# Attention in 512-token chunks inside a rational feed-forward: one activation table set, and the numerator as four matmul terms

## The chip, the cores and the metric

The kernel runs on one core of a Trainium2 chip. The time is device microseconds of the whole program; the kernel before takes 825.4 us (median; 824.55 to 825.59). Some executions fall into a slower state, with a lower granted clock and a longer time; comparisons are between runs of the fast state, unless a text says otherwise. Each ratio is to the kernel before on the same chip and in the same rounds. The twelve experiments ran on four chips, so one experiment set against another may cross chips; the kernel before had medians of 825.00 to 825.28 us on all four. Ratios are the mean time of one kernel's fast runs over that of the other's fast runs of the same rounds, so they are not quite the ratio of the medians quoted beside them.

Engine names in the profile: PE is the matmul engine (PEld its weight loads), ACT is ScalarE, DVE is VectorE, POOL is GpSimd, SP starts the DMAs.

## The reference, cut to what matters

A polynomial-sketch linear attention (batch 4, 4 heads, 1088 positions, head size 32, sketch rank 8) is followed by a feed-forward with a rational activation (4352 tokens, 128 -> 2048 -> 128).

```
phi(x) = outer(S1 x, S2 x), flattened to 64 features
kv = sum over positions of phi(k) v ;  z = sum of phi(k)
x  = (phi(q) kv) / (phi(q) z + 1e-6)              # per head, heads side by side: 128 wide
h  = x @ w_in
P  = a0 + a1 h + a2 h^2 + a3 h^3
Q  = 1 + |b0| |h| + |b1| h^2
out = (P / (Q + 1e-6)) @ w_out
```

1/Q is formed as Exp(-Ln(Q)) in both kernels.

## The kernel before

Attention comes first, in tiles of 128 positions: all keys, then all queries. Its last step writes x, transposed, for all tokens. Then the feed-forward runs in tiles of 1024 tokens, 16 blocks of 128 hidden units each:

```python
for fi in range(nf):
    h_ps = ...                                            # two f32 matmuls of 512 columns
    hh  = copy(h_ps)                                      # ACT, to bf16
    h2  = hh * hh                                         # DVE
    t1  = a1 * hh + a0 ; P3 = a3 * hh + a2                # DVE
    nc.scalar.activation(out=habs, in_=hh, func=ACT.Abs, scale=ab0)
    P   = P3 * h2 + t1                                    # DVE, two instructions
    Qp  = ab1 * h2 + habs                                 # DVE, two instructions
    nc.scalar.activation(out=Qln, in_=Qp, func=ACT.Ln, bias=one_ap)
    nc.scalar.activation(out=Qr, in_=Qln, func=ACT.Exp, scale=-1.0)
    g   = P * Qr                                          # DVE
    out_ps += w_out[fi] x g                               # two bf16 matmuls of 512 columns
```

(Shortened; a scheduler then fixes the order of each engine's instructions before the program runs.)

## Time and profile before

| stage | us | ACT busy | DVE busy | PE busy |
|---|---|---|---|---|
| attention | 0 to 305 | 30% | 36% | 64% |
| feed-forward | 305 to 824 | 97% | 60% | 54% |

The two windows behind the table (length, busy us and count of PE, PEld, DVE, ACT and POOL, granted clock, DMA share, GB/s):

```profile
0.00:305.00 305.00, 196.51 (x746) 132.31 (x746) 110.47 (x251) 91.41 (x388) 9.91 (x55) 1.00 0.17 29
305.00:824.00 519.00, 280.87 (x466) 102.33 (x466) 311.78 (x641) 503.29 (x517) 0.00 (x0) 0.66 0.02 5
```

From the page of the kernel before: the busy lines, and three of the rows that cut the span in 40 slices (each digit is a busy share in tenths; PEclk is the clock granted to PE).

```profile
PE 477.4 (58%) x1212; PEld 234.6 (28%) x1212; DVE 422.3 (51%) x892; ACT 594.7 (72%) x905; POOL 9.9 (1%) x55
...
PE   3888965666565546465665656664555545643331
...
ACT  2222433333332219999999999999999999999997
PEclk9999999999999998777776665567766578555555
...
ACT 57%; PE 21%; issue 10%; DVE 9%; DMA 2%; SPq 0%; ACTq 0%
```

The break at slice 15 is the end of attention. Behind it ACT is full and PE is not, and PE's clock wanders between half and full. The last line is the chain of work that ended last, by engine: more than half of it is ACT.

From the groups of instructions (busy us, mean ns of one), the two lines of table loads:

```profile
L247 ACT ACT_TABLE_LOAD x79 | 101.4, 1283 | 1.5
L245 ACT ACT_TABLE_LOAD x79 | 101.4, 1283 | 1.5
```

And from the timeline, ACT alone, one beat of the feed-forward (start us, duration us, instruction):

```profile
506.84 1.28 ACT L245 ACT_TABLE_LOAD   x1
508.13 1.15 ACT L245 ACTIVATE Qln<-Qp,one_ap 128x1024 bf16<-128x1024 bf16 x1
509.19 1.13 ACT L237 ACTIVATE habs<-hh,b_abs 128x1024 bf16<-128x1024 bf16 x1
510.34 1.28 ACT L247 ACT_TABLE_LOAD   x1
511.63 1.06 ACT L247 ACTIVATE Qr<-Qln 128x1024 bf16<-128x1024 bf16 x1
512.60 0.99 ACT L229 CAST hh<-h_ps 128x1024 bf16<-128x1024 f32 x1
513.61 1.28 ACT L245 ACT_TABLE_LOAD   x1
```

From load to load the beat is 513.61 - 506.84 = 6.77 us, with no gap; 2.56 us of it are two table loads, because Ln and Exp are taken from different sets.

### The profile page before, as it was taken

Reading aid. Unit: us, or ns where it says so; the run is one execution under the profiler, and the core shown is the slowest. Engines: PE = TensorE matmul, PEld = TensorE weight load, DVE = VectorE, ACT = ScalarE, POOL = GpSimd, SP = SyncE. Lnnn points to the kernel's source line nnn. Section 1 sums busy time; section 2 is a strip of 40 time slices with the busy share of each in tenths; the row PEclk is TensorE's granted clock in tenths of the full one; section 3 lists DMA queues with packets and bytes.
Section 4 is the critical chain, followed back from the end, with each engine's and each line's share of the span. In section 5 each row is a group of like instructions: output and inputs, shape, how many; then the busy total and the mean of one; then the engine's idle time right before and its main releaser. Section 6 shows DMA issues by size and latency. Waiting matters only on the chain.

```text
span 824.1 us, 5057 instructions
## 1 busy us (share of the span) xinstructions
PE 477.4 (58%) x1212; PEld 234.6 (28%) x1212; DVE 422.3 (51%) x892; ACT 594.7 (72%) x905; POOL 9.9 (1%) x55
## 2 busy tenths in 40 slices
PE   3888965666565546465665656664555545643331
PEld 2766733333332222121222212221111212211110
DVE  0111344344434446666566665665656666566333
ACT  2222433333332219999999999999999999999997
POOL 3000000000000000000000000000000000000000
PEclk9999999999999998777776665567766578555555
DMA  6333210000000000000000000000000000000000
GB/s 147 59 59 59 33 28 13 8 11 13 5 0 1 0 0 0 1 0 0 0 6 20 0 1 0 0 20 6 0 0 2 13 13 0 0 0 1 19 7 6
DMA packets 59869, 11.34 MB, mean 14 GB/s; under 512 B 54848, under 2 KB 59200, under 8 KB 59712
## 3 DMA queue, kind: packets, MB, share of 16 engines
q1 hardware_dynamic: 59840, 11.02, 7.1%
q8 instruction: 10, 0.16, 0.1%
q14 instruction: 19, 0.16, 0.1%
HBM read 8.79 MB, written 2.23 MB: 13 GB/s over the span
## 4 chain that ended last, share of the span: by engine, by line
ACT 57%; PE 21%; issue 10%; DVE 9%; DMA 2%; SPq 0%; ACTq 0%
ACT L245 12%; ACT L247 11%; ACT Qln L245 10%; ACT Qr L247 8%; ACT hh L229 7%; PE nd_ps L183 5%; DVE denb L197 3%; PE ab_ps L126 3%; ACT xT L188 3%; DVE denb L190 3%; ACT habs L237 2%; PE rden_ps L199 2%; PE q_pT L175 2%; PE ab_ps L165 2%; DVE q_p L169 1%
## 5 line engine op out<-in xcount | busy, mean ns | idle before, releaser
L226 PE MATMUL h_ps<-xT,w_in_sb 128*128 128x512 f32 (+1 forms) x288 | 226.1, 909 | 140.8 <-ACT hh L229 140.4
L226 PEld LDWEIGHTS h_ps<-xT,w_in_sb 128*128 128x128 f32 x288 | 78.1, 293 | 251.9 <-ACT hh L229 205.5
L249 DVE TENSOR_TENSOR g<-P,Qr 128x1024 bf16<-128x1024 bf16 (+1 forms) x80 | 49.0, 612 | 195.7 <-ACT Qr L247 195.7
L252 PE MATMUL out_ps<-g,w_out_sb 128*128 128x512 bf16 (+1 forms) x144 | 66.1, 548 | 81.1 <-DVE g L249 81.0
L188 ACT COPY xT<-nd_ps 32x128 f32<-32x128 f32 (+1 forms) x144 | 35.9, 249 | 105.0 <-PE nd_ps L183 78.1
L247 ACT ACT_TABLE_LOAD x79 | 101.4, 1283 | 1.5
L245 ACT ACT_TABLE_LOAD x79 | 101.4, 1283 | 1.5
L190 DVE COPY denb<-nd_ps 1x128 f32<-1x128 f32 (+1 forms) x144 | 40.6, 282 | 84.6 <-ACT xT L188 83.1
L245 ACT ACTIVATE Qln<-Qp,one_ap 128x1024 bf16<-128x1024 bf16 (+1 forms) x80 | 81.5, 1020 | 2.3 <-DVE Qp L243 1.4
L237 ACT ACTIVATE habs<-hh,b_abs 128x1024 bf16<-128x1024 bf16 (+1 forms) x80 | 80.7, 1008 | 0.1
L247 ACT ACTIVATE Qr<-Qln 128x1024 bf16<-128x1024 bf16 (+1 forms) x80 | 74.1, 928 | 0.9
L229 ACT CAST hh<-h_ps 128x1024 bf16<-128x1024 f32 (+1 forms) x80 | 68.9, 869 | 6.6 <-PE h_ps L226 6.6
L183 PE MATMUL nd_ps<-q_pT_sb,kv_blk 128*128 128x128 f32 (+1 forms) x144 | 52.4, 467 | 21.3 <-DVE denb L190 21.3
L252 PEld LDWEIGHTS <-w_out_sb 128*128 128x128 bf16 x144 | 18.8, 133 | 131.8 <-issue 130.1
L130 DVE TENSOR_TENSOR k_p<-ab_sb 128x256 f32<-128x256 f32 (+1 forms) x36 | 15.3, 425 | 75.0 <-ACT ab_sb L128 75.0
L183 PEld LDWEIGHTS nd_ps<-q_pT_sb,kv_blk 128*128 128x128 f32 x144 | 38.6, 322 | 39.1 <-PE q_pT L175 24.4
L175 PE MATMUL q_pT<-ident,q_p 128*128 128x128 f32 (+1 forms) x72 | 33.0, 458 | 28.8 <-ACT q_pT_sb L179 28.1
L243 DVE TENSOR_TENSOR Qp<-Qp,habs 128x1024 bf16<-128x1024 bf16 (+1 forms) x80 | 48.3, 604 | 0.7 <-ACT habs L237 0.6
L165 PE MATMUL ab_ps<-S12T_blk,kT 128*128 128x64 f32 (+1 forms) x72 | 23.8, 434 | 16.8 <-ACT ab_sb L167 16.0
L128 ACT COPY ab_sb<-ab_ps 128x64 f32<-128x64 f32 (+1 forms) x36 | 7.6, 211 | 32.9 <-PE ab_ps L126 32.9
L126 PE MATMUL ab_ps<-S12T_blk,kT 128*128 128x64 f32 (+1 forms) x72 | 24.0, 436 | 10.7 <-ACT kT L119 10.7
L199 PE MATMUL rden_ps<-denb,hbc 128*128 128x512 f32 (+1 forms) x24 | 18.9, 889 | 18.7 <-DVE denb L197 18.7
(575 smaller groups left out, 614.4 us busy)
## 6 DMA issues: line engine op xcount, KB each, us to landing
out_dram<-outT_sb SPq DMA_DIRECT2D x34, 64.0 KB, 1.6
k_sb<-in_k_dram SPq DMA_DIRECT2D x32, 64.0 KB, 2.3
v_aug<-in_v_dram SPq DMA_DIRECT2D x32, 64.0 KB, 2.1
q_sb<-in_q_dram SPq DMA_DIRECT2D x32, 64.0 KB, 2.1
w_in_sb<-in_moe_w_in_dram SPq DMA_DIRECT2D x1, 1024.0 KB, 5.5
k_sb<-in_k_dram SPq DMA_DIRECT2D x4, 32.0 KB, 2.1
v_aug<-in_v_dram SPq DMA_DIRECT2D x4, 32.0 KB, 2.2
q_sb<-in_q_dram SPq DMA_DIRECT2D x4, 32.0 KB, 2.2
```

The lines of the kernel that those rows point to most:

```text
L126: nc.tensor.matmul(ab_ps[:sl, :], lhsT=kT[:, :sl], rhs=S12T_blk, start=True, stop=True)
L175: nc.tensor.transpose(q_pT[:, :sl], in_=q_p[:sl, 2 * hp:2 * hp + 2, :, :].rearrange("s h i j -> s (h i j)"), identity=ident[:sl, :sl])
L183: nc.tensor.matmul(nd_ps[:, :sl], lhsT=kv_blk_sb[:, blk0:blk0 + wblk], rhs=q_pT_sb[:, :sl], start=True, stop=True)
L188: nc.scalar.copy(out=xT[h * D:(h + 1) * D, tok0:tok0 + sl], in_=nd_ps[off:off + D, :sl])
L190: nc.vector.tensor_copy(out=denb[h * D:h * D + 1, tok0:tok0 + sl], in_=nd_ps[off + D:off + D + 1, :sl])
L226: nc.tensor.matmul(h_ps[:, c0:c0 + cl], lhsT=w_in_sb[:, fi * 128:(fi + 1) * 128], rhs=xT_t[:, c0:c0 + cl], start=True, stop=True)
L229: nc.scalar.copy(out=hh[:, :tl], in_=h_ps[:, :tl])
L237: nc.scalar.activation(out=habs[:, :tl], in_=hh[:, :tl], func=ACT.Abs, scale=ab0)
L245: nc.scalar.activation(out=Qln[:, :tl], in_=Qp[:, :tl], func=ACT.Ln, bias=one_ap)
L247: nc.scalar.activation(out=Qr[:, :tl], in_=Qln[:, :tl], func=ACT.Exp, scale=-1.0)
L249: nc.vector.tensor_mul(out=g[:, :tl], in0=P[:, :tl], in1=Qr[:, :tl])
L252: nc.tensor.matmul(out_ps[:, c0:c0 + cl], lhsT=w_out_sb[:, fi, :], rhs=g[:, c0:c0 + cl], start=(fi == 0), stop=(fi == nf - 1))
```

## The change

The intent: take the table loads and the Abs off ACT, hand the numerator to PE, and hide attention behind the feed-forward. The diff, cut to its core:

```diff
+    nc.scalar.preload_act_table_set("natural_log_exp_and_others")
 ...
-    ST = 128                                  # attention in tiles of 128 positions, all of it first
+    JC = 4; CW = JC * 128                     # attention in chunks of 512 positions
 ...
+            hb = copy(h_ps)                                        # ACT, four blocks of 512 tokens = 2048 columns
+            m = hb & 0x7FFF                                        # |h| as a bit mask, DVE
+            u = b1 * m + b0 ; u = u * m                            # DVE
-            nc.scalar.activation(out=habs[:, :tl], in_=hh[:, :tl], func=ACT.Abs, scale=ab0)
+            nc.scalar.activation(out=L[:, :GW], in_=u[:, :GW], func=ACT.Ln, bias=one_ap)
+            nc.scalar.activation(out=r[:, :GW], in_=L[:, :GW], func=ACT.Exp, scale=-1.0)
-            nc.vector.tensor_mul(out=g[:, :tl], in0=P[:, :tl], in1=Qr[:, :tl])
+            ys = [r]
+            for t in range(1, 4):                                  # r h, r h^2, r h^3
+                nc.vector.tensor_mul(out=y[:, :GW], in0=ys[-1][:, :GW], in1=hb[:, :GW])
+            for t in range(4):                                     # W_terms[t] = a[t] * w_out, in bf16
+                for i in range(gf):
+                    nc.tensor.matmul(out_ps[:, :W], lhsT=W_terms[t][:, fi, :], rhs=ys[t][:, i * W:(i + 1) * W], ...)
+            for f in fill[g::ng]:                                  # pieces of the next chunk's attention
+                f()
 ...
+    for f in key_pieces(0) + main_query(0, 0, xs):                 # the start: keys of batch 0, first query chunk
+        f()
+    for n, (b, c) in enumerate(chunks):                            # 8 chunks of 512 tokens
+        fill = main_query(*chunks[n + 1], xs) + (key_pieces(b + 1) if c == 0 else [])   # shortened
+        moe_chunk(xs[n], CW, GF, fill, store_main(b, c))
+    moe_chunk(xs[len(chunks)], B * REM, 2 * GF, [], store_rem)     # the 4 x 64 positions left over
```

The query's features are now made transposed, by two f32 matmuls of 512 columns per pair of heads (A and B) and one product; the division is done before the transpose. Inputs come in fewer, larger DMAs.

## The prediction

> **What bounds it now.** Two stages in series. The windows by stage show attention from 0 to 305 us; no engine is full there (ACT about 30%, DVE 34%), it is a chain of small tiles, and the 853 ns between f32 passes of 512 columns is that of a half-speed PE. The feed-forward fills 305 to 824 us with ACT 98 to 99% busy from 330 to 800. The timeline shows its beat: one 128x1024 tile takes 6.77 us of ACT: copy 1.00, Ln 1.15, Abs 1.14, Exp 1.06, two table loads of 1.28. The groups show 158 such loads, 203 us, and 81 us of Abs. The Trainium skill, "ScalarE: Activation LUTs", section "Table sets", says one set holds Exp and Ln; the trace agrees with that page's 1283 ns per load and shows two switches per tile.
>
> **What the change does.** One load instead of 159; Abs becomes a bit mask on DVE. Feed-forward ACT per 1024 columns falls to about 2.9 us (copy 0.95, half of a 2048-wide Ln and Exp, extrapolated to 2.0 and 1.9). Attention is batched in 512-token chunks, and the scheduled order puts its pieces between the groups of the feed-forward; only the first keys and query chunk stay ahead. The cost goes to PE: 64 bf16 output matmuls per 512 tokens instead of 16.
>
> Estimate per 512-token chunk, full-speed PE, from pitches in the trace:
> - PE: 16 f32 matmuls of 512 columns x 0.853 = 13.7; 64 bf16 x 0.215 = 13.8; query pieces 6.7; keys 2.9 on average. Sum 37 us.
> - DVE: four groups of mask 0.6, u 0.7, four bf16 products of 2048 at 1.13 = 23.4; attention about 5. Sum 28 us.
> - ACT: eight copies 7.6, four Ln and Exp 15, six 512-column copies 3.3, keys 1. Sum 27 us.
>
> So the bound moves from ACT to PE. Eight chunks and a half one: 8 x 37 + 14 = 310 us of PE work.
>
> **What lies on the critical path.** All of the feed-forward's ACT saving, down to PE's own time; nearly all of attention but a start of about 30 us (loads, keys of batch 0, first query). I add stalls of 5.5 us per chunk: ACT delivers Exp every 5.0 to 5.4 us while PE has 4 to 5 us of work; the products come at 1.13 us while PE eats one in 0.86; the query chain gates the next chunk's h. I add 12 us for three key chunks, 5 for ramping up, 3 for the half chunk, 10 for the last group's chain and store. 30 + 8 x 42.5 + 14 + 12 + 5 + 3 + 10 = 414; as some overlap, I say 405.
>
> **Prediction: 405 us, 370 to 445 eight times in ten.** Faster by over 2%: 0.985; within 2%: 0.005; slower: 0.01.
>
> **What would show each step right or wrong.** Page, busy line: PE about 80%, ACT and DVE 55 to 70%. Groups: one table load; 544 output matmuls at about 215 ns. Chain that ended last: PE in front. Slices: PEclk 9 or more after the start; PE 8 or 9 from 30 us on. Windows: about 43 us per chunk. Waits: output matmuls on the products and on Exp.
>
> **What would make it wrong.** The granted clock: before, PE flips between half and full in the feed-forward (0.50 to 0.91 by window). I assume PE is busy enough to stay above 0.9; at half speed a chunk costs 74 us; at 0.75, about 450 us in all. A mask at half the rate I assume would put DVE level with PE. A scheduled order that fits the chip badly would stretch every chunk.

## The result, and the profile after

The changed kernel takes 388.89 us (386.75 to 389.04, four runs) against 825.4 us: ratio 0.4706, interval 0.4695 to 0.4717. The prediction was 405, with a range of 370 to 445.

The same lines of the page, after:

```profile
PE 353.5 (91%) x1407; PEld 185.0 (48%) x1429; DVE 254.8 (66%) x345; ACT 227.9 (59%) x211; POOL 7.7 (2%) x29
...
PE   3987999999998999899969999999999998998873
...
ACT  2110494559817971489543955469569916981970
PEclk9999999999999999999987999999999999999998
...
PE 62%; DVE 20%; ACT 13%; issue 3%; DMA 1%; SPq 0%; DVEq 0%; ACTq 0%
```

PE is now full and its clock stays up. ACT is no longer full, but its row is not even: slices at 9 stand beside slices at 4. That unevenness matters below. The table loads, in the groups:

```profile
L50 ACT ACT_TABLE_LOAD x1 | 1.3, 1283 | 0.7 <-PEq L383 0.7
```

The windows by stage (length, busy us and count of each engine, granted clock, DMA share, GB/s): the start up to the first matmul of the feed-forward, the eight chunks, and the last half chunk.

```profile
core 0: us, PE busy (x) PEld busy (x) DVE busy (x) ACT busy (x) POOL busy (x), PEclk, DMA share, GB/s
0.00:39.60 39.60, 29.66 (x101) 21.47 (x102) 13.38 (x34) 5.79 (x11) 6.62 (x27) 1.00 0.63 183
39.60:357.00 317.40, 304.06 (x1191) 149.50 (x1213) 224.07 (x295) 205.32 (x186) 1.10 (x2) 0.99 0.03 11
357.00:387.00 30.00, 19.74 (x117) 13.99 (x116) 17.32 (x17) 16.77 (x14) 0.00 (x0) 0.97 0.05 14
```

A chunk takes 317.4 / 8 = 39.7 us, where the prediction had about 43. Its work is close to the predicted sums: 38.0 us of PE, 28.0 of DVE and 25.7 of ACT, for 37, 28 and 27. PE is busy for 91% of the span and not for about 80%. (The clock of 1.00 in the first window is not a measurement; e5 below shows why.)

### The profile page after: what moved, and what is told of

It is laid out like the page before. It is cut to its first block, busy times and chain, and to the rows that moved or that the text cites. A ratio compares the mean times of both kernels' runs of the same rounds, so it can differ in the third digit from the quotient of the medians.

```text
span 387.1 us, 3609 instructions
## 1 busy us (share of the span) xinstructions
PE 353.5 (91%) x1407; PEld 185.0 (48%) x1429; DVE 254.8 (66%) x345; ACT 227.9 (59%) x211; POOL 7.7 (2%) x29
## 4 chain that ended last, share of the span: by engine, by line
PE 62%; DVE 20%; ACT 13%; issue 3%; DMA 1%; SPq 0%; DVEq 0%; ACTq 0%
PE out_ps L307 20%; PE h_ps L285 18%; PE w_ps L231 5%; PE kv_ps L188 5%; PE w_ps L236 5%; ACT L L296 5%; DVE u L294 4%; PE w_ps L243 4%; ACT hb L287 3%; DVE u L292 2%; PE w_ps L171 2%; DVE m L289 2%; PE w_ps L166 1%; DMA in_k_dram<-in_k_dram 1%; ACT xT L260 1%
## 5 line engine op out<-in xcount | busy, mean ns | idle before, releaser
L285 PE MATMUL h_ps<-xT,w_in_sb 128*128 128x512 f32 (+1 forms) x288 | 136.1, 598 | 6.9 <-ACT xT L260 4.2
L287 ACT CAST hb<-h_ps 128x1024 bf16<-128x1024 f32 x68 | 67.4, 1015 | 45.4 <-PE h_ps L285 44.5
L285 PEld LDWEIGHTS h_ps<-xT,w_in_sb 128*128 128x128 f32 x288 | 52.8, 196 | 56.5 <-issue 33.2
L296 ACT ACTIVATE L<-u,one_ap 128x2048 f32<-128x2048 bf16 x34 | 68.5, 2015 | 16.3 <-DVE u L294 16.2
L289 DVE TENSOR_SCALAR m<-hb 128x2048 int16<-128x2048 int16 x34 | 23.4, 688 | 37.4 <-ACT hb L287 37.4
L294 DVE TENSOR_TENSOR u<-u,m 128x2048 bf16<-128x2048 bf16 x34 | 41.8, 1230 | 0.5
L292 DVE TENSOR_SCALAR u<-m,b_abs 128x2048 bf16<-128x2048 bf16 x34 | 27.5, 809 | 0.6
L307 PEld LDWEIGHTS <-w_out_297 128*128 128x128 bf16 x144 | 13.6, 98 | 23.6 <-issue 13.3
L307 PEld LDWEIGHTS <-w_out_295 128*128 128x128 bf16 x144 | 13.9, 98 | 20.3 <-issue 9.2
L307 PEld LDWEIGHTS <-w_out_293 128*128 128x128 bf16 x144 | 14.0, 99 | 20.2 <-issue 8.8
L307 PEld LDWEIGHTS <-w_out_291 128*128 128x128 bf16 x144 | 13.9, 99 | 17.5 <-issue 8.7
L231 PE MATMUL w_ps<-qT,Srep_158 64*128 64x512 f32 (+1 forms) x36 | 21.2, 672 | 0.7 <-ACT qT L225 0.7
L236 PE MATMUL w_ps<-qT,Srep_162 64*128 64x512 f32 (+1 forms) x36 | 20.3, 645 | 0.7 <-ACT A_sb L234 0.7
L188 PE MATMUL kv_ps<-v_aug,k_p 128*128 128x66 f32 x128 | 20.0, 308 | 0.6 <-DVE k_p L180 0.6
```

The lines of the kernel that those rows point to most:

```text
L188: nc.tensor.matmul(kv_tiles[b][:, hp * 66:(hp + 1) * 66], lhsT=k_rows[:, hp * 128:(hp + 1) * 128], rhs=v_rows[:, 2 * hp:2 * hp + 2, :], st ...
L231: nc.tensor.matmul(A_ps[:, :W], lhsT=Srep[0][rows].rearrange("p g f -> p (g f)"), rhs=st["qT"][rows, :W], start=True, stop=True)
L236: nc.tensor.matmul(B_ps[:, :W], lhsT=Srep[1][rows].rearrange("p g f -> p (g f)"), rhs=st["qT"][rows, :W], start=True, stop=True)
L285: nc.tensor.matmul(h_ps[:, i * W:(i + 1) * W], lhsT=w_in_sb[:, fi * 128:(fi + 1) * 128], rhs=xT[:, :W], start=True, stop=True)
L287: nc.scalar.copy(out=hb[:, s * W:(s + nsub) * W], in_=h_ps)
L289: nc.vector.tensor_scalar(out=m[:, :GW].bitcast(mybir.dt.int16), in0=hb[:, :GW].bitcast(mybir.dt.int16), scalar1=0x7FFF, scalar2=None, op0 ...
```

## The experiments

Two theories went in. Mine: the old time was ACT's loads plus a serial attention, and the new time is PE's work, with ACT and DVE having some 10 us of slack in each chunk of 37 us. The rivals: one part of the change carries nearly everything; or the new kernel is bound by a chain of latencies (copy, mask, Ln, Exp, products) and PE is merely busy.

All twelve runs gave results that passed the comparison with the reference. The medians are over all executions of a run; in e4, e8, e9 and e10 one of the four was slow, and the median of the fast ones alone is 359.2, 344.6, 370.9 and 420.5. e9 and e12 are built on e7, e10 on e5, e11 on e8.

| run | what | median us | ratio to before |
|---|---|---|---|
| e1 | before + one table set | 623.2 | 0.7553 |
| e2 | after without the set | 474.6 | 0.5755 |
| e3 | after, numerator on DVE | 405.1 | 0.4910 |
| e4 | after, bf16 x and w_in | 359.9 | 0.4358 |
| e5 | after, attention first | 473.3 | 0.5736 |
| e6 | after + ACT copies in the place of loads | 449.3 | 0.5441 |
| e7 | after, x made earlier | 376.5 | 0.4563 |
| e8 | e4 + earlier x + deeper buffers | 344.6 | 0.4176 |
| e9 | e7 + useless matmuls in the start | 371.9 | 0.4501 |
| e10 | e5 + useless matmuls in attention | 421.3 | 0.5100 |
| e11 | e8 + useless matmuls in the start | 338.55 and 340.69 (fast), 345.87 and 346.71 (slow) | not given |
| e12 | e7 + the copies of e6 | 450.5 | 0.5478 |

### e1: the old kernel with one table set

```diff
+    nc.scalar.preload_act_table_set("natural_log_exp_and_others")
     ST = 128
```

> The old kernel with one line added, that fixes the table set; nothing else. Theory (the feed-forward was bound by ScalarE, two thirds of a load and an Abs too many per tile): the 158 loads go, ScalarE falls from 6.77 to about 4.2 us per tile, and VectorE (4.2 us busy per tile before) takes over at 4.4 to 5.0 us: 650 to 690 us. Rival (the loads were hidden or the gain came from the new structure alone): over 780 us. Rival 2 (the loads alone carry most of the gain): under 600 us.

Measured 623.24 us. The saving is 825.02 - 623.24 = 201.8 us, and 158 loads x 1.283 are 202.7 us: practically all of the loads' time had been paid. The result lies between my 650 to 690 and the second rival's under 600. DVE did take over, but without waits. The windows of e1, the middle of its feed-forward:

```profile
330.00:600.00 270.00, 179.70 (x408) 68.71 (x407) 269.78 (x534) 252.94 (x302) 0.00 (x0) 0.86 0.03 7
```

DVE is busy for 269.78 of 270 us and ACT for 252.94: with the loads gone the two are nearly level, so the close match of 201.8 and 202.7 is in part chance. In the old structure, one line of the change is worth nearly half of the whole gain of 436 us; e2 has what it is worth in the new one.

### e2: the new kernel without the set

```diff
-    nc.scalar.preload_act_table_set("natural_log_exp_and_others")
```

> The new kernel without the line that fixes the set: 68 loads of 1.28 us come back, 87 us of ScalarE work. Theory (PE is the bound at 37 to 40 us per chunk, ScalarE has 27): ScalarE goes to about 37 us per chunk, level with PE, and waits for Exp grow: 405 to 435 us. Rival (ScalarE is off the path, its slack swallows the loads): within 2% of the new kernel, under 397. Rival 2 (the loads are paid in full): 476.

Measured 474.56 us, 85.7 us more than the new kernel. The 68 loads add 87.2 us of ACT work, so nearly all is paid, although ACT is busy for only 68% of this run. This hit the second rival and missed my 405 to 435: ACT's slack could not be used. The instruction orders may explain part of it: apart from the loads, the ACT order of e2 is that of the new kernel, all 210 instructions, and PE's and DVE's differ only by a few instructions in the start. So the order was made as if there were no loads, and PE waits in that order. PE's two largest waits by their totals, in the new kernel, then in e2 (engine, what waited, for whom: us in total, times, longest):

```profile
PE h_ps L285 <- ACT xT L260: 4.2, 4, 1.5
PE w_ps L258 <- DVE x_sb L250: 3.1, 3, 1.7
```

```profile
PE out_ps L306 <- ACT r L297: 27.0, 22, 2.3
PE h_ps L284 <- ACT hb L286: 19.0, 11, 2.1
```

In the new kernel PE waits almost nowhere. In e2 the output matmuls wait for Exp, up to 2.3 us at a time, near the 2.57 us of two loads.

### e3: the numerator on DVE, one output matmul per block

```diff
-            ys = [r]                      # and three products, four terms on PE
+            h2 = hb * hb ; t1 = a1 * hb + a0 ; P = a3 * hb + a2
+            P = P * h2 ; P = P + t1 ; P = P * r      # all on DVE
+            ys = [P]                      # one term; w_out in bf16, not scaled
```

> The new kernel with the polynomial formed on VectorE as before and one output matmul per block instead of four. PE loses 408 bf16 matmuls of 0.215 us, 88 us; VectorE gains three instructions per group, about 88 us, and reaches some 343 us busy. Theory: the bound moves from PE to VectorE and the time stays near: 385 to 415 us. Rival (four terms on PE were a clear gain, as PE was idle): over 430. Rival 2 (PE is the only bound that matters): under 340.

Measured 405.1 us, as expected: 4% slower than with four terms. PE was relieved of 408 matmuls x 0.215 = 88 us, yet its busy time fell only from 353.5 to 311.8 us, as the granted clock fell from 0.989 to 0.822; DVE rose to 331.3 us (82%). In this kernel the four terms on PE are worth 16 us.

### e4: x and w_in in bf16

```diff
-            xT = xpool.tile([128, CW], FP, name="xT")
+            xT = xpool.tile([128, CW], BF, name="xT")
 ...
+        nc.vector.tensor_copy(out=w_in_bf, in_=w_in_sb)          # once, at the start
 ...
-                    nc.tensor.matmul(h_ps[...], lhsT=w_in_sb[...], rhs=xT[:, :W], ...)
+                    nc.tensor.matmul(h_ps[...], lhsT=w_in_bf[...], rhs=xT[:, :W], ...)
```

> The new kernel with x and w_in in bf16 for the first matmul: 136 f32 matmuls go from 0.853 to 0.215 us each, PE loses about 87 us, all else is the same. Theory (PE is the bound): PE falls to 27 us per chunk, level with VectorE (28) and ScalarE (27): 310 to 340 us. Rival (the critical path is the latency of copy, mask, Ln, Exp and products, and PE is merely busy): over 370 us. The error of the result may grow; the output must still pass the comparison.

Measured 359.9 us: 29 us saved of 87 us taken from PE. Both theories missed. Of the 87 us at full speed, PE's busy time fell by 64 (353.5 to 289.2), because the clock fell to 0.921, and its idle time rose by 35 (33.6 to 68.2); 64 - 35 is the 29 that remained. The largest of the new waits is again that of output matmuls on Exp:

```profile
PE out_ps L310 <- ACT r L301: 20.6, 9, 6.6
```

So PE's work was a bound, but relieving it made gaps. That the gaps are what lowered the clock is argued here, not shown.

### e5: attention first

```diff
-        moe_chunk(xs[n], CW, GF, fill, store_main(b, c))
+        for f in fill:
+            f()
+    one = ...                       # 1.0, computed from the last x
+    w_in_sb = w_in_sb * one         # no matmul of the feed-forward can start before
+    for n, (b, c) in enumerate(chunks):
+        moe_chunk(xs[n], CW, GF, [], store_main(b, c))
```

(Nine buffers for x, and w_out loaded through a buffer of the feed-forward, to make room.)

> The new kernel with the interleaving undone: all keys and queries first, in the same batched pieces, and w_in is held back until the last x is there, so that no matmul of the feed-forward can start before; x is kept in nine buffers and w_out is loaded through a buffer of the feed-forward to make room. Work is the same. Theory (interleaving hides attention's chain): attention alone takes 120 to 170 us, as PE idles and runs at half speed there, the feed-forward alone 260 to 290 us: 400 to 460 us in all. Rival (PE's work is the bound and adds up to the same wherever it stands): within 3% of 389.

Measured 473.3 us, 84 us more; somewhat over my range. Attention takes 205.6 us here (305 in the kernel before) and the feed-forward 265.4 us (519 before). The windows:

```profile
0.00:205.60 205.60, 168.24 (x531) 112.19 (x531) 51.07 (x143) 29.17 (x57) 8.09 (x29) 1.00 0.15 43
205.60:471.00 265.40, 248.46 (x882) 113.32 (x898) 207.02 (x205) 202.55 (x154) 0.00 (x0) 0.99 0.03 9
```

PE looks 82% busy in attention, and PEclk says 1.00. Both mislead. The line of the query matmul A in the answers by line (its 36 records: shortest, median, longest duration in ns; first and last start), in e5 and then in the new kernel:

```profile
L231 PE MATMUL w_ps<-qT,Srep x36: 631/1054/1216, 22.9 to 199.4; 64*128 64x512 f32 x32, 64*128 64x256 f32 x4
```

```profile
L231 PE MATMUL w_ps<-qT,Srep_158 x36: 376/641/1219, 23.0 to 352.8; 64*128 64x512 f32 x32, 64*128 64x256 f32 x4
```

The same instruction takes 1054 ns in one place and 641 in the other. An f32 matmul stands in the trace as two records, its two passes. From the first to the second it is 853 or 1015 ns in e5, and 429 or 533 ns in the new kernel's chunks: about half speed against full. The PEclk row shows full speed before the first recorded change, whatever the speed was: in e5's packed trace the first clock entry, a rise to full, stands at 208.9 us, 3 us after the feed-forward began. (In the kernel before it stands at 311.2 us, in the new kernel at 43.8.)

### e6: ACT copies where the loads stood

```diff
+            nc.scalar.copy(out=junk, in_=u[:, :1316])
             nc.scalar.activation(out=L[:, :GW], in_=u[:, :GW], func=ACT.Ln, bias=one_ap)
+            nc.scalar.copy(out=junk, in_=L[:, :1316])
             nc.scalar.activation(out=r[:, :GW], in_=L[:, :GW], func=ACT.Exp, scale=-1.0)
```

> The new kernel with one table set, and before each Ln and each Exp a useless ScalarE copy of 1316 columns of that instruction's own input, estimated at 1.28 us from the trace: the same ScalarE work in the same places as the 68 table loads of the run without the set (which cost 85.7 us of the 87 added, in the very order of instructions of the new kernel). The difference: the scheduler sees these copies when it orders the instructions, and did not see the loads. Theory (the loads are paid in full because the order is fixed without them, each output matmul standing just where its Exp is due): a good part is absorbed, 400 to 445 us. Rival (a chain of latencies through ScalarE bounds the kernel, whatever the order): 465 us or more.

The copies took what was meant, as the groups of e6 show:

```profile
L299 ACT CAST junk<-L 128x1316 bf16<-128x1316 f32 x34 | 43.8, 1289 | 0.0
L296 ACT COPY junk<-u 128x1316 bf16<-128x1316 bf16 x34 | 43.8, 1289 | 31.2 <-DVE u L294 27.4 <-DVE den L248 3.6
```

Measured 449.3 us: the same ACT work costs 60 us when the scheduler can order around it, and 86 when it cannot. 449 lies between the ranges of the two theories. The 26 us of difference are what the order made with the copies in view was worth here; e12 below, with another such order, pays 74, so they are no clean measure of what blindness costs.

### e7: x made earlier

```diff
-            for f in fill[g::ng]:
+            for f in (fill[2 * g:2 * g + 2] if g < ng - 1 else fill[2 * g:]):
```

> The new kernel with the four query pieces of the next chunk placed behind groups 0 and 1 instead of behind groups 0 to 3. Theory (the order falls into bursts of first matmuls, with ScalarE waiting, and runs of output matmuls, with PE paced by Exp, because the next x comes only at the end of a chunk): an earlier x mixes them and saves 5 to 20 us: 369 to 384. Rival (PE is 90% occupied already, the order leaves nothing): within 1.5% of 389.

Measured 376.5 us, ratio 0.4563, inside the expected 369 to 384: 3% faster than the new kernel by moving the query pieces. (Where a chunk also has key pieces or loads, the same line moves those behind groups 2 and 3.) PE's idle time falls from 33.6 to 25.7 us, all of it in the chunks:

```profile
40.00:347.00 307.00, 301.65 (x1212) 150.97 (x1231) 224.93 (x296) 206.94 (x188) 1.10 (x2) 1.00 0.03 12
```

There 13.3 us of idle PE (317.40 - 304.06) become 5.4. The number was right, but the mechanism that I had expected is not what the traces show. In the new kernel's PE order, bursts of up to 12 first matmuls alternate with runs of up to 47 recorded output matmuls without one (attention's own matmuls and the last half chunk left aside); in e7 the longest are again 12 and 47. What has gone are the waits for x itself: in the new kernel's chunks PE waits 4.2 us for the copy to xT and 2.5 for x_sb (the two lines shown at e2 are for the whole span), and in e7's chunks no wait on xT is listed, and on x_sb only

```profile
PE w_ps L258 <- DVE x_sb L250: 0.5, 1, 0.5
```

So the gain is, for the most part, an x that is there in time, and not a better mixture.

### e8: bf16, the earlier x and five buffers for hb

```diff
+            (the edits of e4 and e7; w_in and w_out loaded through buffers of L, to make room)
-            hb = moe.tile([128, GF * CW], BF, name="hb", bufs=3)
+            hb = moe.tile([128, GF * CW], BF, name="hb", bufs=5)
```

> The kernel with bf16 x and w_in (359.9 us), with the early x of the run beside it and five instead of three buffers for hb (w_in and w_out are loaded through the buffers of L to make room). Theory (that kernel gave back 58 of the 87 us of PE time because of bursts): 315 to 345 us. Rival (latency from copy to product bounds it): 352 to 365.

Measured 344.6 us (three fast runs of 344.48 to 344.65, one slow of 360.3), at the very edge of my range. Against e4, the earlier x and the buffers gave 15 us more; how the two share it was not tested. This is faster than both kernels (ratio 0.4176). Its x and w_in are rounded to bf16.

### e9 and e10: useless matmuls where PE waits

```diff
+    def heat(src, n=4):                       # results are never read
+        t = hps.tile([128, 1024], FP, name="h_ps")
+        for _ in range(n):
+            nc.tensor.matmul(t[:, :w], lhsT=ident_bf, rhs=<bf16 halves of src>, start=True, stop=True)
+    heat(ident, 24)
 ...
+        heat(kT)      # behind the key matmuls
+            heat(qT)  # behind A and B
+            heat(q_pT) # behind the numerator matmuls
```

In e9 they stand in the start only, in e10 in all of attention.

> The kernel with the early x (376.5 us) plus useless bf16 matmuls in the start only: 24 on the identity, then four after each step of the first keys and query, placed where PE waits for a copy or a product; their results are never read. Before them the first 40 us run at half speed by the passes (853 ns for 512 columns, 429 later). Theory (the start is slow because PE's gaps keep its clock at half): the clock rises, passes fall to 427 ns, the first matmul of the feed-forward starts at 28 to 35 us instead of 39.6: 365 to 373 us. Rival (the start's time is loads, copies and products, or the gaps are not what holds the clock): the extra matmuls cost 0 to 10 us: 376 to 387.

> The kernel with attention in front (473.3 us; attention to 205 us, at half speed throughout by its passes) with the same useless matmuls in all its pieces. Theory (interleaving paid by keeping PE's clock up as much as by overlap): passes fall to about 429 ns and attention ends at 140 to 170 us in place of 205: 410 to 440 us. Rival (overlap alone, the clock stays at half): attention gets longer by the added matmuls, 475 us or more.

e9 measured 370.5 to 372.9 us in its three fast runs (ratio 0.4501 against 0.4563 for e7; a fourth, slow one took 381.5). The first matmul of the feed-forward starts at 35.0 us instead of 39.3. The line of A in the start, in e7 and then in e9:

```profile
L231 PE MATMUL w_ps<-qT,Srep x4: 1054/1135/1216, 22.9 to 30.5; 64*128 64x512 f32 x4
```

```profile
L246 PE MATMUL w_ps<-qT,Srep x4: 589/641/693, 22.8 to 29.5; 64*128 64x512 f32 x4
```

e10 measured 421.3 us (fast runs 419.9 to 422.2), 52 us less than e5, by adding work whose results nobody reads. Its profile is of a run in the slow state (426.8 us), so only the passes, the clock's entries and the start of the feed-forward are read from it:

```profile
L246 PE MATMUL w_ps<-qT,Srep x36: 375/590/1216, 24.8 to 153.7; 64*128 64x512 f32 x32, 64*128 64x256 f32 x4
```

The median fell from 1054 to 590 ns. The first clock entry of this trace, a rise to full, stands at 9.8 us, 4 us after the first useless matmul (5.8 us). In that profile the feed-forward starts at 158.8 us in place of 205.7. So of the 84 us that the interleaving is worth, 52 can be had without any overlap, by a higher clock in attention; the other 32 hold what overlap gives and what the useless matmuls cost, which was not separated.

In e5, between 40 and 200 us, no single wait of PE was over 0.9 us; the longest group of waits there is

```profile
PE w_ps L243 <- DVE q_pT L239: 12.5, 15, 0.9
```

so short gaps are enough to hold the clock down (PE is idle for 25.6 of the 165 us from 40 to 205 us; in e10 for 7.6 of the 118 us from 40 to 158), or it is the kind of work: these are f32 passes of few columns with many weight loads, and the useless matmuls were dense bf16. Which of the two it is was not separated.

### e11: the same in the start of e8

> The fastest kernel so far (344.6 us) with the same useless matmuls in its start. Theory: 333 to 341 us; rival: 344 to 355.

Inconclusive in size: two runs were fast (338.55 and 340.69 us) and two slow. The fast ones are 4 to 6 us under those of e8, in the direction of e9 and inside the expected 333 to 341.

### e12: the copies of e6 with the earlier x

> The kernel with the early x (376.5 us) with the 68 useless ScalarE copies of 1.29 us that cost the new kernel 60 us of their 88 (388.9 to 449.3). Theory (that cost comes from bursts, in which ScalarE and PE take turns at being the bound; an earlier x mixes them): the copies cost clearly less here, under 40 us: below 417 us. Rival (ScalarE's latency between a first matmul and its output matmul is part of a loop that no order loosens): 55 to 65 us again, 431 to 442.

Measured 450.5 us: the copies cost 74 us here, more than the 60 of e6 and above the range of the rival too. The theory that bursts make ACT's work count, and that an earlier x cures it, has fallen. PE in five profiles, each span split into busy and idle (span minus busy; a few matmul records can be missing from a trace):

| profile | span | PE busy | PE idle | clock |
|---|---|---|---|---|
| after | 387.1 | 353.5 | 33.6 | 0.989 |
| e2 | 471.3 | 381.3 | 90.0 | 0.947 |
| e6 | 452.0 | 379.5 | 72.5 | 0.939 |
| e7 | 374.4 | 348.7 | 25.7 | 0.993 |
| e12 | 447.2 | 372.1 | 75.1 | 0.953 |

The added ACT time shows up twice: as waits (e12 over e7: 49 us of PE idle) and as slower passes (23 us of PE busy, with the same matmuls, at a lower clock). The waits of PE in e12 name what it waits for:

```profile
PE out_ps L310 <- ACT r L301: 40.3, 21, 5.8
PE out_ps L310 <- DVE r L305: 6.3, 22, 1.3
```

It is Exp. Why no order absorbs more, with ACT idle for 31% of e12, stays open. It fits a loop through two engines that run strictly in order (a group's output matmuls wait for its Exp, the next first matmuls stand behind them on PE, and ACT's next copy waits for those), but no run here broke such a loop (the copies of e12 with more buffers for hb would be one test), so this is argued and not shown.

## Why the prediction was right or wrong

- **The old bound: right.** ACT's loads were on the path: 201.8 us saved by e1 for 202.7 us of loads.
- **Where the gain came from.** By the stages of e5, batching took attention from 305 to 205.6 us (about 100), the feed-forward fell from 519 to 265.4 (about 254, of which the table set alone gives 202 in the old structure), and interleaving gave 84. The three add up to the gain by construction, so their sum confirms nothing; what e5 shows is the length of each stage.
- **The new bound moves to PE: right, with a limit.** PE is 91% busy and leads the chain with 62%. But I had read ACT's 27 us of work in a chunk with 37 of PE as slack, and it was not: 87 us of ACT work cost 86 (e2), or 60 and 74 when the scheduler saw it (e6, e12). And 87 us off PE saved only 29 (e4). Near this point every engine's work counts for something.
- **The start: mis-sized.** I said 30 us; it took 39.6. I had read the half speed of PE in the old attention, but did not apply it to the new start; e9 got 4 us of it back, all after the first query matmul, which starts at 22.9 us in e7 and at 22.8 in e9. The other 5 us of the error stay unexplained.
- **The stalls: mis-sized the other way.** I added 5.5 us per chunk, 1.5 for key chunks, and 5 for ramping up; the chunks took 317.4 us where I had 340 + 12 + 5 = 357. With my 37 us of work per chunk, 2.7 us of stalls are left. I had named waits of the output matmuls on Exp and the products; in the new kernel such waits hardly exist (the longest is 1.1 us). Other work stands before them in PE's order.
- **The end: about right.** 14 + 3 + 10 = 27 us, measured 30.
- **The clock condition: right.** It had to stay above 0.9, and it stayed at 0.99 in the chunks. The feed-forward keeps that clock by itself (0.99 in e5 too). What the prediction missed is attention: alone its matmuls run at about half speed, and between those of the feed-forward at full speed. e10 got 52 us back by clock without interleaving; that the interleaving owes the same 52 us to it is argued.

The terms added up to 414, and 9 us were taken off "as some overlap". The start's error (10 us too little) and the stalls' error (40 us too much) have opposite signs, so it is partly luck that 405 came as near to 388.9 as it did.

What the pages say, against these runs. The Trainium skill, "ScalarE: Activation LUTs", section "Table sets", says that one set holds both Exp and Ln; e1 agrees: one load, a correct result. The Trainium skill, "VectorE: DVE Perf Modes", section on the perf-mode tiers, gives 693 ns for a one-source bf16 instruction of 2048 columns and 1224 for a two-source one; the mask on int16 measured 688 ns and the product 1230, but u = b1 * m + b0, one-source with two scalars per partition, 809. The Trainium skill, "TensorE: Matmul & The Clock Gate", Part 1, says the default is the throttled state and activity releases it; e10 agrees, 1054 to 590 ns. The Trainium skill, "Trainium Kernel Development and Optimization", section "Performance Expectations", warns that matmul busy time is a bad metric, because matmuls are pipelined; e5 shows it misleading for another reason as well, 82% busy in attention at half speed.

## What to carry to other kernels

Before rewriting a stage that one engine fills, ask what that engine does besides work: here one line that fixed the table set gave 202 us of 825 in the old kernel. Read PE's speed from the spacing of equal passes and not from its busy share or the clock row; where it is half, dense work beside it (another stage, or even useless matmuls) can make the stage itself faster. When the busiest engine is at 90%, do not count the others' idle time as slack until a run has added work to them.

## What the Trainium skill lacked or had wrong

- "ScalarE: Activation LUTs", section "What ACT_TABLE_LOAD costs", has 1283 ns for the load plus about 1380 ns of drain for each switch, 2.66 us in total. The load is right (1283 ns). No such drain shows: in the beat of the kernel before, a load starts 0.02 us after the end of the instruction before it, and the next one starts 0.01 us after the load. Two such instructions without a load between them overlap by 0.09 us, so a load costs about 1.4 us in all (an estimate from these four figures).
- "TensorE: Matmul & The Clock Gate", section on HAM oscillation, states the rule as no PE gaps over about 3.4 us. In e5 PE ran at half speed for some 160 us without a wait over 0.9 us. The rule alone is not enough for streams of small f32 matmuls. (The page's next section knows short idles that disturb the clock, but in bf16 matmuls of 512 columns and as an oscillation.)
- The same page, "Back-to-back issue gap", has 131 ns per matmul of 512 columns sustained with a weight load each. The output matmuls here, each with its own weights, stand 215 to 216 ns apart at full speed, which is the page's figure for the isolated gap.
- "FP8 and Floating Point Precision", section "TensorE Precision Notes", counts four passes for a true f32 matmul; no page gives its time or says how a profile shows it. Here one of 512 columns and 128 rows is two records 429 ns apart at full speed (853 at half), each twice the 215 ns of a bf16 matmul.
- "TensorE: Matmul & The Clock Gate" warns that clock events in a trace can be unreliable, but no page says that the granted clock in a profile like this one reads as full before its first recorded change: 1.00 in e5's attention, at half speed by the passes, with the first entry at 208.9 us.
- "ScalarE: Activation LUTs" says that the compiler's back end puts the table loads in; it does not say that an order of instructions fixed before leaves them out of account. Here the order of ACT's 210 instructions is the same with and without 68 loads, which cost 86 us; 68 ACT copies of the same length that the scheduler saw cost 60 (e6) and 74 (e12).
